# Edge columns of a convolution left out, input loads moved to another queue, statistics rows put in fewer DMAs, and second-phase expansions spread out, in a ConvNeXt-V2 block

## Chip, cores and metric

The kernel runs on one core of a Trainium2 chip. The metric is device time in microseconds (us), the median of several executions. No slow run occurred, and all kernels gave the reference's result. Ratios: the mean time of one kernel's runs over the mean of the other's of the same rounds, with a 95% interval; that is not quite the ratio of the medians that are quoted beside it.

The engines are called TensorE (PE in the profile, PEld its weight loads), VectorE (DVE), ScalarE (ACT), GpSimd (POOL) and SyncE (SP). SyncE does no arithmetic here: it only issues DMAs.

## The reference, cut to what matters

```python
# x: (1, 512, 512, 96) bf16; dw: (3, 3, 96); w1: (96, 384); w2: (384, 96)
xp = jnp.pad(x, ((0,0),(1,1),(1,1),(0,0)))
out = sum(xp[:, i:i+H, j:j+W, :] * dw[i, j] for i, j in 3x3)   # depthwise convolution
h = layernorm(out, axis=-1)
h = gelu_tanh(h @ w1)                                           # 384 channels
gx = sqrt((h * h).sum(axis=(1, 2)) + 1e-6)                      # over all pixels: GRN
nx = gx / (gx.mean(axis=-1) + 1e-6)
h = gamma * (h * nx) + beta + h
return x + h @ w2
```

The sum over all pixels splits the work in two. Phase 1 must see the whole picture before any output can be made; phase 2 multiplies by `w2`, whose rows by then carry the scale.

## The kernel before

The picture is cut into 128 blocks of 4 rows (2048 pixels). Phase 1 runs one *slot* for each block, software-pipelined: load x, transpose it, 3x3 convolution as 32x32 diagonal matmuls, statistics, normalization, a trip of the normalized block `yn` through DRAM to change its layout, expansion to 384 channels, gelu, sums of squares. For most blocks the gelu output is made again in phase 2 from `yn`; for the others it is stored (`g_dram`). The parts that the change and the argument touch:

```python
        def load_x(b):
            t = xinpool.tile([128, SL, C], bf16, name="xin")
            off = x.offset + b * GR * W * C
            if b in (0, NBLK - 1):
                pool.memset(t[:, 0:SL:SL - 1, :], 0.0)
        # ... (cut)
            else:
                act.dma_start(out=t[:].rearrange("p g c -> p (g c)"),
                              in_=bass.AP(x.tensor, off - C, [[PXP * C, 128], [1, SL * C]]))
            xins[b] = t

        def turn_x(b):
            xin = xins.pop(b)
            t = xt_ring[b % NXT]
            pairs = t[:, 0:2, :].rearrange("p i s -> p (i s)").bitcast(f32)
            dve.transpose(out=pairs.rearrange("p (g m) -> p g m", m=MB),
                          in_=xin[:, :, 0:64].bitcast(f32))
            dve.transpose(out=t[:, 2, :].rearrange("p (g m) -> p g m", m=MB), in_=xin[:, :, 64:96])
            flat = t[:].rearrange("p i s -> p (i s)")
            n = SL * MB
            for c0, c1 in ((0, 2), (2 * n - 2, 2 * n + 1), (3 * n - 1, 3 * n)):
                pool.memset(flat[:, c0:c1], 0.0)
        # ... (cut)

            def tap(n):
                k = sum(len(ms) for ms in mms[:n])
                mm = None
                for j, a, i, dx in mms[n]:
                    r = b * GR + j + a - 1
                    q = r % GR
                    c0 = MB * (1 + dx)
                    if mm is None and n in (3, 6):
                        pe.drain()
                    mm = pe.matmul(
                        Y[32 * j:32 * j + 32, i, :],
                        lhsT=Wd[32 * q:32 * q + 32, i, 3 * a + dx + 1, :],
                        rhs=x_row(r // GR, q, i, c0),
                        start=first[i, j] == k,
                        stop=last[i, j] == k,
                    )
                    k += 1
```

`load_x` issues its DMA from ScalarE. `turn_x` lets GpSimd zero the edge columns of the transposed block; the taps of the convolution (`tap`) read 512 columns from it.

Each batch of four blocks has its reciprocal standard deviations written to DRAM as rows (four DMAs) and read back as a broadcast, again four DMAs, one for each row of the blocks, 32 partitions each. `stage_write` stores `yn`, with the 4 rows as the slowest dimension of the DRAM side; `stage_read` brings it back with 96 channels on the partitions.

```python
        def stage_rows(k):
            b0, n = BATCHES[k]
            rt = rts.pop(k)
            N = n * GR * NG
            dst = r_dram[b0:b0 + n].rearrange("b r (g m) -> (b r g) m", g=NG)
            nq = min(32, N)
            with nc.allow_non_contiguous_dma("small rows of rstd"):
                for a in range(4):
                    sp.dma_start(
                        out=dst[:, 32 * a:32 * a + 32].rearrange("(t q) p -> q t p", q=nq),
                        in_=rt[32 * a:32 * a + nq, :(N + 31) // 32 * 32].rearrange("q (t p) -> q t p", p=32))

        def stage_bcast(k):
            b0, n = BATCHES[k]
            rbc = rbcpool.tile([128, BATCH, W], bf16, name="rbc")
            for j in range(GR):
                sp.dma_start(out=rbc[32 * j:32 * j + 32, :n, :],
                             in_=r_dram[b0:b0 + n, j, :].partition_broadcast(32))
            rbcs[k] = rbc
        # ... (cut)
        def stage_write(b):
            sp.dma_start(out=yn_dst(b), in_=yns.pop(b)[:])

        def stage_read(b):
            t = yn_ring[b % NYT]
            sp.dma_start(out=t[:C], in_=yn_src(b))
            ynts[b] = t
```

In the slot loop, all stores of a finished block (up to three of 512 KB) are issued together:

```python
        for s in range(last_slot + 1):
            get = lambda kind: at.get((s, kind), [])
            for b in get("write"):
                stage_write(b)
            for b in get("read"):
                stage_read(b)
            for k in get("bcast"):
                stage_bcast(k)
            if s + 3 < NBLK:
                load_x(s + 3)
            for f in stores:
                f()
            stores = []
        # ... (cut)
                b = mlp[0]
                expand, expand_px, squares, store = mlp_units(b)
                if pm_rows(b):
                    us = [lambda j=j: expand(j, 0) for j in range(NCH)] + [lambda n=n: expand_px(n) for n in range(3)]
                else:
                    us = [lambda j=j, i0=i0: expand(j, i0) for j in range(NCH) for i0 in (0, 2)]
                for f in bursts[0]:
                    f()
                us[0]()
                us[1]()
                squares(0)
                stores.append(lambda f=store: f(0))
                for f in bursts[1]:
                    f()
```

In phase 2 a recomputed block has its four expansions (three matmuls of 512 columns and one gelu each) made one block ahead, in the gaps of the block before; the loads are issued from GpSimd, SyncE and ScalarE.

```python
            g = gld.tile([128, NCH, GR * W], bf16, name="gl")
            ynt = None
            if not is_recomp(q):
                for j in range(NCH):
                    (nc.gpsimd, nc.sync, nc.scalar)[j].dma_start(out=g[:, j, :], in_=g_dram[q, j])
            else:
                ynt = ynld.tile([C, GR, W], bf16, name="ynl")
                nc.scalar.dma_start(out=ynt[:], in_=yn_src(q))
            xr = xrpool.tile([128, PXP, C], bf16, name="xr")
            nc.gpsimd.dma_start(out=xr[:], in_=x[0, r0:r0 + GR].rearrange("r w c -> (r w) c").rearrange(
                "(p g) c -> p g c", g=PXP))
            grp[q] = dict(g=g, ynt=ynt, xr=xr)
        # ... (cut)
        def stage_mm2(q, units):
            g, xb = grp[q]["g"], grp[q]["xb"]
            o_sb = opool.tile([128, PXP, C], bf16, name="o_sb")
            for sub in range(NSUB):
                O = psO.tile([128, GPS, C], f32, name="O")
                for gl_ in range(GPS):
                    gg = sub * GPS + gl_
                    for j in range(NCH):
                        nc.tensor.matmul(O[:, gl_, :], lhsT=g[:, j, gg * 128:(gg + 1) * 128], rhs=W2s[:, j, :],
                                         start=(j == 0), stop=(j == NCH - 1))
                nc.vector.tensor_tensor(out=o_sb[:, sub * GPS:(sub + 1) * GPS, :], in0=O[:],
                                        in1=xb[:, sub * GPS:(sub + 1) * GPS, :], op=ALU.add)
                if units:
                    units.pop(0)()
            grp.pop(q)
            return o_sb
        # ... (cut)
        PRE = 4
        nth = lambda n: ORDER[n] if n < NBLK else None
        for n in range(min(PRE, NBLK)):
            stage_load(ORDER[n])
        stage_xb(ORDER[0])
        for u in recompute_units(nth(0)):
            u()
        held = None
        for n, q in enumerate(ORDER):
            if n + PRE < NBLK:
                stage_load(ORDER[n + PRE])
            stage_xb(nth(n + 1))
            o_sb = stage_mm2(q, recompute_units(nth(n + 1)))
            if held:
                stage_out(*held)
            held = (q, o_sb)
        stage_out(*held)
```

## Time and profile before

| | before |
|---|---|
| median of 3 runs (lowest to highest) | 1909.8 us (1894.3 to 1910.1) |
| convolution stage of phase 1 (first to last evacuation of a convolution) | 25.7 to 1173.7 us, 9.04 us a slot |
| end of phase 1 ("drain": last blocks, final statistics) | 1173.7 to 1274.1 us, 100 us |
| phase 2 | 1274.1 to 1905.3 us, 631 us |

The first fence is from the page of the profiled run. Part 1 gives busy time, share of the span and number of instructions for each engine. Part 2 cuts the span into 40 slices: a digit is the busy share in tenths, PEclk the granted clock of TensorE in tenths of full speed, DMA the busy share of the 16 DMA engines, GB/s what they moved.

```profile
PE 1574.0 (83%) x28354; PEld 911.0 (48%) x28354; DVE 1152.7 (60%) x2022; ACT 1356.5 (71%) x1227; POOL 1381.3 (73%) x1355
...
PEclk9889989998999989999989999989999999999999
DMA  3346666665666666666566654569999999999995
GB/s 79 104 149 188 204 198 194 206 210 182 213 201 202 189 213 191 226 220 191 197 212 205 209 188 161 199 213 317 316 317 312 317 312 308 313 310 314 313 318 195
...
q10 hardware_dynamic: 34272, 111.16, 18.4%
```

About two thirds of the span (slices 1 to 26) move some 200 GB/s at a DMA share of 0.6; the rest moves 313 GB/s at 0.9 to 0.95. These are the two phases. q10 is ScalarE's queue; the others, not shown, are those of SyncE (q1) and GpSimd (q0).

The next fence is the table of stretches: the stretch, its length, busy us of each engine with the number of instructions, then granted clock, DMA share and GB/s. The first row is the whole convolution stage, the second 200 us of phase 2.

```profile
core 0: us, PE busy (x) PEld busy (x) DVE busy (x) ACT busy (x) POOL busy (x), PEclk, DMA share, GB/s
25.70:1173.70 1148.00, 965.91 (x20538) 512.90 (x20537) 784.15 (x1292) 796.77 (x793) 844.36 (x1020) 0.93 0.60 192
1400.00:1600.00 200.00, 170.63 (x2275) 113.31 (x2273) 85.61 (x162) 156.27 (x115) 155.55 (x95) 1.00 0.95 313
```

TensorE is busy 965.9 of 1148 us in the convolution stage, and idle 182 us. No other engine is fuller.

What the engines waited for between 200 and 1000 us (who waited, for whom, total us, times, longest us):

```profile
POOL yn L34 <- DMA rbc<-r_dram: 54.0, 11, 6.9
PE U L34 <- ACT gt L34: 53.6, 54, 3.5
ACT gt L34 <- DMA r_dram<-rt: 29.6, 11, 5.0
ACT gt L34 <- DMA yn_dram<-yn: 27.4, 4, 7.1
PE Y L34 <- POOL xT L34: 24.0, 16, 2.8
```

ScalarE's gelu (`ACT gt`) waits for two DMAs here that it has no data from (and for two more, 14.3 and 10.5 us, further down the list). They are waits of its own x loads, which stand ahead of the gelu in ScalarE's order: in the trace 111 of the 132 load instructions have waits for one or two of eight DMA semaphores before them, on which the `yn` stores, the rstd rows and other transfers land too. The timeline of ScalarE around one such stall (start, us, engine, operation; in brackets the idle time before it and what ended it):

```profile
612.92 1.96 ACT L34 ACTIVATE gm<-U 128x1024 bf16<-128x1024 f32 x2
621.52 0.36 ACTq L34 DMA_DIRECT2D xin<-in_x_dram  x1
621.98 1.94 ACT L34 ACTIVATE gt<-U 128x1024 bf16<-128x1024 f32 x2 [7.10 <-DMA yn_dram<-yn]
```

The x load could be issued only at 621.52, when a `yn` store had landed, and the gelu behind it started 7.10 us late.

### The profile page before, as it was taken

How to read it: one execution, taken by the hardware profiler on the slowest of the kernel's cores; microseconds unless marked ns; L12 is line 12 of the kernel's file. 1: busy time of each engine (PE TensorE's matmuls, PEld its weight loads, DVE VectorE, ACT ScalarE, POOL GpSimd, SP SyncE). 2: the span in 40 equal slices, each digit the busy share in tenths (PEclk: the TensorE clock that was granted, in tenths of full speed). 3: DMA queues.
4: the chain of work that ended last, by engine and by line, in shares of the span. 5: the costliest groups of instructions: out<-in, count | busy, mean ns of one | idle time of the engine just before them, and what ended most of it. 6: DMA issues, size and time to landing. Idle time of an engine off the chain costs nothing.

```text
span 1905.3 us, 64704 instructions
## 1 busy us (share of the span) xinstructions
PE 1574.0 (83%) x28354; PEld 911.0 (48%) x28354; DVE 1152.7 (60%) x2022; ACT 1356.5 (71%) x1227; POOL 1381.3 (73%) x1355
## 2 busy tenths in 40 slices
PE   5788888888898889888888878658888888888887
PEld 2334444444454445444444444335555555555555
DVE  5356766776677677767867767774444444444444
ACT  0165777776777778777767768857777877777776
POOL 4667777687777777867767876447777777777775
PEclk9889989998999989999989999989999999999999
DMA  3346666665666666666566654569999999999995
GB/s 79 104 149 188 204 198 194 206 210 182 213 201 202 189 213 191 226 220 191 197 212 205 209 188 161 199 213 317 316 317 312 317 312 308 313 310 314 313 318 195
DMA packets 188634, 433.75 MB, mean 228 GB/s; under 512 B 31712, under 2 KB 97344, under 8 KB 188352
## 3 DMA queue, kind: packets, MB, share of 16 engines
q1 hardware_dynamic: 138528, 248.98, 39.0%
q10 hardware_dynamic: 34272, 111.16, 18.4%
q0 software_dynamic: 15552, 69.48, 11.8%
q8 instruction: 222, 3.64, 0.8%
q14 instruction: 60, 0.49, 0.1%
HBM read 268.59 MB, written 160.96 MB: 225 GB/s over the span
## 4 chain that ended last, share of the span: by engine, by line
PE 27%; ACT 25%; DMA 20%; DVE 11%; POOL 7%; issue 5%; SPq 2%; ACTq 1%; POOLq 0%; DVEq 0%
ACT gl L696 12%; PE O L724 10%; DMA ynT<-yn_dram 8%; DVE bst L34 7%; ACT gl L703 6%; PE U L34 6%; ACT gt L34 5%; PE Y L34 5%; DMA yn_dram<-yn 5%; DMA rbc<-r_dram 4%; PE U L694 3%; PE SG L34 3%; POOL yn L34 2%; SPq L34 2%; DVE xT L34 2%
## 5 line engine op out<-in xcount | busy, mean ns | idle before, releaser
L34 DVE BATCH_NORM_STATS2 bst<-gt 128x6 f32<-128x512 bf16 x984 | 602.2, 674 | 296.3 <-ACT gt L34 295.9
L34 ACT ACTIVATE gt<-U 128x1024 bf16<-128x1024 f32 x492 | 478.3, 1028 | 269.2 <-PE U L34 113.9
L726 DVE TENSOR_TENSOR o_sb<-O,xb 128x384 bf16<-128x384 f32 x512 | 271.9, 555 | 355.7 <-PE O L724 355.5
L696 ACT ACTIVATE gl<-U 128x1536 bf16<-128x1536 f32 x264 | 374.9, 1455 | 152.7 <-PE U L694 152.7
L712 POOL TENSOR_TENSOR xb<-xr,B2bc_f 128x1536 f32<-128x1536 bf16 x126 | 393.0, 3119 | 100.6 <-DVE o_sb L726 99.4
L34 PE MATMUL Y<-xT,Wd 32*32 32x512 bf16 x13806 | 384.8, 408 | 92.7 <-POOL xT L34 35.2
L34 POOL TENSOR_TENSOR yn<-y_bf,rbc 128x1536 bf16<-128x1536 bf16 x128 | 396.6, 3100 | 87.9 <-DMA rbc<-r_dram 82.9
L34 PE MATMUL U<-ynT,w1p 128*128 128x512 bf16 x1008 | 294.6, 398 | 92.4 <-ACT gt L34 79.6
L34 POOL TENSOR_TENSOR ysq<-y_bf 128x1536 bf16<-128x1536 bf16 x128 | 351.9, 2750 | 16.2 <-ACT y_bf L34 16.2
L724 PEld LDWEIGHTS <-gl 128*128 128x128 bf16 x6048 | 285.6, 98 | 152.2 <-ACT gl L703 92.1
L724 PE MATMUL O<-W2s,gl 128*128 128x96 bf16 x6048 | 313.2, 206 | 49.4 <-ACT gl L703 48.8
L34 PEld LDWEIGHTS <-Wd 32*32 32x32 bf16 x13806 | 163.1, 90 | 284.7 <-issue 233.0
L34 ACT ACTIVATE gm<-U 128x1024 bf16<-128x1024 f32 x264 | 261.0, 1034 | 11.0 <-PE U L34 10.9
L694 PE MATMUL U<-ynl,w1p 96*128 96x512 bf16 x792 | 226.9, 379 | 42.3 <-ACT gl L696 40.2
L34 ACT ACTIVATE y_bf<-Y 128x1536 bf16<-128x1536 f32 x105 | 152.8, 1455 | 87.0 <-PE Y L34 70.1
L34 PEld LDWEIGHTS <-w1p 128*128 128x128 bf16 x1008 | 81.9, 99 | 252.7 <-issue 205.8
L34 DVE STREAM_TRANSPOSE xT<-xin 128x576 f32<-128x576 f32 (+1 forms) x256 | 181.3, 748 | 0.0
L34 PE MATMUL U<-w1p,ynT 128*128 128x384 bf16 (+2 forms) x1056 | 159.9, 287 | 20.1 <-ACT gt L34 12.4
L34 POOL MEMSET xT<- 128x2 bf16 (+2 forms) x384 | 26.5, 103 | 199.0 <-DVE xT L34 197.2
L34 PEld LDWEIGHTS <-ynT 128*128 128x128 bf16 x1056 | 90.7, 102 | 112.4 <-issue 83.2
L34 PE MATMUL SG<-gm 128*128 128x128 bf16 x2112 | 134.5, 221 | 0.8 <-issue 0.8
L703 ACT ACTIVATE gl<-U 128x1536 bf16<-128x1536 f32 x88 | 128.2, 1457 | 0.0
(83 smaller groups left out, 926.9 us busy)
## 6 DMA issues: line engine op xcount, KB each, us to landing
g_dram<-gt SPq DMA_DIRECT2D x114, 512.0 KB
xin<-in_x_dram ACTq DMA_DIRECT2D x126, 432.0 KB
yn_dram<-yn SPq DMA_DIRECT2D x128, 384.0 KB
ynT<-yn_dram SPq DMA_DIRECT2D x128, 384.0 KB
out_dram<-o_sb SPq DMA_DIRECT2D x128, 384.0 KB
xr<-in_x_dram POOLq DMA_DIRECT2D x126, 384.0 KB, 5.3
ynl<-yn_dram ACTq DMA_DIRECT2D x88, 384.0 KB
gl<-g_dram SPq DMA_DIRECT2D x38, 512.0 KB
```

The lines of the kernel that those rows point to most:

```text
L34: r = f(*a, **k)
L694: nc.tensor.matmul(U[:, i, :], lhsT=w1p[:C, j * 128:(j + 1) * 128], rhs=ynt[:, i, :], start=True, stop=True)
L696: nc.scalar.activation(out=perm_view(g[:, j, :], 0, 3), in_=perm_src(U[:]), func=ACTF.Gelu_apprx_tanh)
L703: nc.scalar.activation(out=g[:].rearrange("p j (g r m) -> p r j g m", g=PXP, r=GR, m=MB)[:, 3], in_=perm_src(U[:]), func=ACTF.Gelu_apprx_tanh)
L712: nc.gpsimd.tensor_tensor(out=xb[:], in0=grp[q]["xr"][:], in1=B2bc_f[:, None, :].to_broadcast([128, PXP, C]), op=ALU.add)
L724: nc.tensor.matmul(O[:, gl_, :], lhsT=g[:, j, gg * 128:(gg + 1) * 128], rhs=W2s[:, j, :], start=(j == 0), stop=(j == NCH - 1))
L726: nc.vector.tensor_tensor(out=o_sb[:, sub * GPS:(sub + 1) * GPS, :], in0=O[:], in1=xb[:, sub * GPS:(sub + 1) * GPS, :], op=ALU.add)
```

## The change

The change has six parts, in two phases.

1. Edge columns of the convolution are left out: taps at the left and right edge write 511 columns, so GpSimd's three memsets per block (384 in all) go away.
2. x loads move from ScalarE's queue to SyncE's.
3. The rstd rows of a batch go out in two DMAs for four, and come back in **one** broadcast DMA for four ("2+1").
4. Stores of gelu blocks are issued one a slot.
5. In phase 2 no load is issued from ScalarE.
6. In phase 2 the expansions are spread evenly over all blocks, a whole block (four units) ahead, with TensorE, VectorE and ScalarE held to program order. Blocks are loaded five ahead for four, into six buffers for five.

The diff also gives half-size gelu tiles of phase 1 a pool of their own (`gth` for `gt`), which is not shown here.

The diff, cut to its core:

```diff
-                act.dma_start(out=t[:].rearrange("p g c -> p (g c)"),
+                sp.dma_start(out=t[:].rearrange("p g c -> p (g c)"),
                               in_=bass.AP(x.tensor, off - C, [[PXP * C, 128], [1, SL * C]]))
... (cut)
-            flat = t[:].rearrange("p i s -> p (i s)")
-            n = SL * MB
-            for c0, c1 in ((0, 2), (2 * n - 2, 2 * n + 1), (3 * n - 1, 3 * n)):
-                pool.memset(flat[:, c0:c1], 0.0)
... (cut)
+                    o0, o1 = max(0, -dx), W - max(0, dx)
+                    c0 = MB * (1 + dx) + o0
                     if mm is None and n in (3, 6):
                         pe.drain()
                     mm = pe.matmul(
-                        Y[32 * j:32 * j + 32, i, :],
+                        Y[32 * j:32 * j + 32, i, o0:o1],
                         lhsT=Wd[32 * q:32 * q + 32, i, 3 * a + dx + 1, :],
-                        rhs=x_row(r // GR, q, i, c0),
+                        rhs=x_row(r // GR, q, i, c0, o1 - o0),
                         start=first[i, j] == k,
                         stop=last[i, j] == k,
... (cut)
-            dst = r_dram[b0:b0 + n].rearrange("b r (g m) -> (b r g) m", g=NG)
-            nq = min(32, N)
+            nq, nt = min(32, N), (N + 31) // 32
             with nc.allow_non_contiguous_dma("small rows of rstd"):
-                for a in range(4):
-                    sp.dma_start(
-                        out=dst[:, 32 * a:32 * a + 32].rearrange("(t q) p -> q t p", q=nq),
-                        in_=rt[32 * a:32 * a + nq, :(N + 31) // 32 * 32].rearrange("q (t p) -> q t p", p=32))
+                if nq == 32:
+                    for t in range(nt):
+                        sp.dma_start(
+                            out=r_dram[b0:b0 + n].rearrange("b r w -> (b r w)").rearrange(
+                                "(t q a p) -> t a q p", q=32, a=4, p=32)[t],
+                            in_=rt[:, 32 * t:32 * t + 32])
... (cut)
-            for j in range(GR):
-                sp.dma_start(out=rbc[32 * j:32 * j + 32, :n, :],
-                             in_=r_dram[b0:b0 + n, j, :].partition_broadcast(32))
+            sp.dma_start(out=rbc[:, :n, :].rearrange("p n w -> p (n w)"),
+                         in_=bass.AP(r_dram[b0].tensor, r_dram[b0].offset, [[n * W, GR], [0, 32], [1, n * W]]))
... (cut)
-            for f in stores:
-                f()
-            stores = []
+            if stores:
+                stores.pop(0)()
... (cut)
             else:
                 ynt = ynld.tile([C, GR, W], bf16, name="ynl")
-                nc.scalar.dma_start(out=ynt[:], in_=yn_src(q))
+                nc.sync.dma_start(out=ynt[:], in_=yn_src(q))
             xr = xrpool.tile([128, PXP, C], bf16, name="xr")
... (cut)
-                if units:
-                    units.pop(0)()
+                        pe2.matmul(O[:, gl_, :], lhsT=g[:, j, gg * 128:(gg + 1) * 128], rhs=W2s[:, j, :],
+                                   start=(j == 0), stop=(j == NCH - 1))
+                dve2.tensor_tensor(out=o_sb[:, sub * GPS:(sub + 1) * GPS, :], in0=O[:],
+                                   in1=xb[:, sub * GPS:(sub + 1) * GPS, :], op=ALU.add)
+                pace(n, sub)
... (cut)
-        PRE = 4
+        PRE = 5
+        UPB = NCH + 1
+        LEAD = UPB
+        todo = [n for n, q in enumerate(ORDER) if is_recomp(q) for _ in range(UPB)]
+        total = len(todo)
+        made = [0]
+        waiting = []
+
+        def advance(target, upto):
+            while made[0] < total and made[0] < target and todo[made[0]] < upto:
+                n = todo[made[0]]
+                if not waiting:
+                    waiting.extend(recompute_units(ORDER[n]))
+                waiting.pop(0)()
+                made[0] += 1
+
+        def pace(n, sub):
+            due = sum(1 for v in todo if v <= n + 1) if sub == NSUB - 1 else 0
+            even = LEAD + (n * NSUB + sub + 1) * total / (NSUB * NBLK)
+            advance(max(due, even), n + PRE)
+
... (cut)
-        for u in recompute_units(nth(0)):
-            u()
+        advance(LEAD, PRE)
```

## The prediction

> **What bounds it now.** Two phases. Phase 1 (conv, norm, expansion, statistics; 0 to 1260 us) runs slots of about 9.1 us (66 squares on GpSimd in 600 us, the table of stretches). TensorE is busy 85% there at a granted clock of 0.94, ScalarE 75%, VectorE 72%, GpSimd 74%. Phase 2 (1290 to 1905 us) has TensorE 85%, ScalarE 78%, the DMA engines 95% at 313 GB/s.
>
> In phase 1 the DMA share is only 0.64, but the packet records show a lopsided load: three or more packets are in flight 96% of the time, with peaks at 4 to 5 and at 16. The yn store (4x96x512 against 128 partitions) moves its 1 KB packets with about a quarter of the engines busy. [...] So four "hot" engines carry every yn store. By the median packet times (1 KB 46 ns, 3456 B 135 ns, 4 KB 159 ns), their work per slot, an estimate: yn store 96x46 = 4.4 us, xin 1.1, ynT 0.95, g 1.1, rstd broadcast 0.4: 8.0 us of 9.1, or about 95% with the slow packets in the mean. Long landings (yn store up to 13 us) stall ScalarE through its own DMA issues (list of waits: gelu behind r_dram, ynT, yn_dram, rbc: about 125 us), and TensorE waits 92 us for gelu.
>
> **What the change does.**
> - Edge memsets: 384 x 103 ns leave GpSimd, with its 197 us of waiting for the transposes, and TensorE's 35 us wait for them. Conv columns 511 for 512: nothing.
> - ScalarE loses its DMA stalls (up to 125 us, of which TensorE saw perhaps 60).
> - g stores are spread: fewer 1.5 MB bursts.
> - The rstd broadcast becomes one DMA whose source has slowest dimension 4[...]. Per batch of 4 slots: 32 packets of 4 KB x 159 ns = 5.1 us for 32 x 46 ns = 1.5 us before; rows add 0.4. So the hot engines get about 1.0 us more per slot: 9.0 us at median packet times (estimate), nearer 9.7 with slow packets. This is a floor: what ScalarE and GpSimd gain cannot be collected, and phase 1 becomes bound by four DMA engines: +65 us.
> - Startup: xin is issued after 19 SyncE loads (10 us of issues): included, about +7 us.
> - Phase 2: expansions a block ahead take away TensorE's waits for gelu (49 + 40 us). But the DMA engines are at 95%; 5% of 600 us is all there is: -25 us.
>
> Sum: 1909.8 + 65 - 25 = 1950 us; 80% range 1875 to 2030. Faster by over 2%: 0.17; within 2%: 0.33; slower: 0.50.
>
> **What would show it.** Right: slot 9.4 to 9.9 us; the broadcast's packets 4 KB with a quarter of the engines; concurrency 4 to 5 more often; ScalarE's waits for DMA gone, but VectorE's transposes or TensorE's expansions waiting for xin or ynT; SyncE lagging. Phase 2 about 590 us with DMA 97% or more and the waits for gelu small. Wrong: broadcast on 16 engines, slot below 8.8 us, granted clock nearer 1.
>
> **What would make it wrong.** If slow packets come from two queues interleaving, one queue may be quicker and phase 1 stays at 9.1 us or falls; if the broadcast spreads over 16 engines, phase 1 gains 60 us or more; if phase 2's DMA can go above 330 GB/s, it gains up to 50 us; if one in-order queue delays xin behind waiting issues, it is slower still.

The sum came to 1909.8 + 65 - 25 = 1950 us. Two things in it were the author's estimate: that the merged broadcast would move on a quarter of the engines, and that this would be the same quarter that carries the `yn` stores (its "hot engines"). The 1.0 us more a slot, and with it the +65, rest on both. For the `yn` store the trace of before shows the quarter: from 667.75 to 668.75 us, with mostly 4 of its 1 KB packets in flight and hardly anything else, the DMA share is 0.27. For the broadcast the trace of after shows it, below. No trace numbers the engines.

## The result

| | before | after |
|---|---|---|
| median us (lowest to highest, 4 runs each) | 1909.95 (1894.3 to 1910.9) | 1833.71 (1818.95 to 1840.3) |
| convolution stage | 1148.0 us, 9.04 a slot | 1107.6 us, 8.72 a slot |
| drain | 100.4 us | 122.6 us |
| phase 2 | 631.2 us | 573.5 us |
| mean granted clock over the span | 0.955 | 0.949 |

The ratio is 0.961 (0.953 to 0.969): faster by about 4%, 75 us of span. The predicted 1950 us was on the wrong side; the range began at 1875. About 18 us came from phase 1 and 58 us from phase 2. About 6 us of the longer drain lie in the new program order: expansions stand ahead of the first output matmul on TensorE, which starts at 1256.4 though the scale was summed at 1248.5 (7.9 us later; before, 1.6 us).

The same parts of the page after:

```profile
PE 1536.7 (84%) x28172; PEld 922.8 (50%) x28354; DVE 1163.8 (64%) x2022; ACT 1366.3 (75%) x1227; POOL 1358.4 (74%) x971
...
PEclk9899999999999989999999999897999999999998
DMA  3355666666666666665666665558999999999983
GB/s 82 99 153 190 206 214 193 207 219 217 201 210 203 205 199 209 206 210 196 214 216 202 208 205 178 169 200 255 359 379 369 351 343 337 360 375 365 356 290 133
```

ScalarE's queue q10, 18.4% of the engines' span before, is gone from the page. Most slices of phase 2 now show 337 to 379 GB/s, where before they stood at 308 to 318.

The table of stretches after (same columns; the trace lacks some 170 matmul records of the convolution stage, about 8 us of busy time at 46 ns each):

```profile
core 0: us, PE busy (x) PEld busy (x) DVE busy (x) ACT busy (x) POOL busy (x), PEclk, DMA share, GB/s
26.20:1133.80 1107.60, 941.93 (x20366) 507.18 (x20538) 783.97 (x1289) 798.27 (x793) 820.08 (x644) 0.95 0.60 196
1400.00:1600.00 200.00, 181.78 (x2563) 132.51 (x2561) 98.90 (x183) 174.19 (x126) 175.71 (x105) 0.97 1.00 350
```

The waits after, 200 to 1000 us:

```profile
POOL yn L34 <- DMA rbc<-r_dram: 183.4, 22, 9.9
...
DVE xT L34 <- DMA xin<-in_x_dram: 80.7, 30, 5.6
...
PE Y L34 <- DVE xT L34: 49.0, 24, 4.9
```

TensorE's 53.6 us of waiting for gelu have become 1.6 (further down this list), and its 24 us for the edge memsets are gone. In their place VectorE's transposes wait 80.7 us for x itself, TensorE 49.0 us for the transposes, and the normalization on GpSimd 183.4 us for the rstd broadcast (54.0 before). So the old stalls were removed and a new one was made: data now comes late on SyncE's queue. Two stretches of 2 us show the new broadcast in flight:

```profile
720.00:722.00 2.00, 1.79 (x43) 0.84 (x42) 0.66 (x2) 1.97 (x3) 0.00 (x0) 1.00 0.26 107
722.00:724.00 2.00, 2.00 (x45) 1.78 (x44) 0.00 (x0) 2.00 (x3) 0.00 (x0) 1.00 0.28 112
```

The DMA share (second number from the right) is 0.26 to 0.28 while the broadcast moves: a quarter of the engines carry it, and the packet records show 4 KB packets there. That is the quarter that the prediction had counted on. Which engines they are, the trace doesn't show. But from 722.25 to 724 us packets of an x load (3456 B) are in flight beside those of the broadcast, and even so only 4 or 5 of SyncE's queue are in flight together.

### The profile page after: what moved, and what is told of

It reads as the page before. It is cut to its first block, busy times and chain, and to the rows that moved or that the text cites. A ratio compares the mean times of both kernels' runs of the same rounds, so it can differ in the third digit from the quotient of the medians.

```text
span 1829.9 us, 63713 instructions
## 1 busy us (share of the span) xinstructions
PE 1536.7 (84%) x28172; PEld 922.8 (50%) x28354; DVE 1163.8 (64%) x2022; ACT 1366.3 (75%) x1227; POOL 1358.4 (74%) x971
## 4 chain that ended last, share of the span: by engine, by line
POOL 40%; issue 20%; PE 17%; DMA 13%; ACT 5%; DVE 3%; SPq 1%; another core or an unknown queue 0%; ACTq 0%; DVEq 0%; POOLq 0%
POOL yn L34 17%; POOL ysq L34 17%; PE O L34 9%; PE U L34 8%; DMA out_dram<-o_sb 6%; ACT gl L34 4%; DMA gl<-g_dram 4%; POOL nt L34 3%; POOL var L34 2%; DVE bst L34 2%; DMA rbc<-r_dram 1%; DMA yn_dram<-yn 1%; PE Y L34 1%; DVE o_sb L34 1%; POOL rn L34 1%
## 5 line engine op out<-in xcount | busy, mean ns | idle before, releaser
L34 ACT ACTIVATE gl<-U 128x1536 bf16<-128x1536 f32 x352 | 489.9, 1450 | 94.5 <-PE U L34 89.0
L34 ACT ACTIVATE gth<-U 128x1024 bf16<-128x1024 f32 x264 | 261.0, 1025 | 200.2 <-issue 154.3
L34 PEld LDWEIGHTS <-gl 128*128 128x128 bf16 x6048 | 301.6, 99 | 148.4 <-ACT gl L34 41.1
L34 PE MATMUL O<-W2s,gl 128*128 128x96 bf16 x6048 | 324.8, 209 | 55.7 <-ACT gl L34 30.2
L34 DVE BATCH_NORM_STATS2 bst<-gth 128x6 f32<-128x512 bf16 x528 | 326.0, 671 | 50.9 <-ACT gth L34 50.8
L34 PE MATMUL U<-ynT,w1p 128*128 128x512 bf16 x851 | 285.2, 406 | 49.8 <-DMA ynT<-yn_dram 14.5
L34 DVE BATCH_NORM_STATS2 bst<-gt 128x6 f32<-128x512 bf16 x456 | 276.2, 676 | 78.5 <-ACT gt L34 78.4
L34 PE MATMUL U<-ynl,w1p 96*128 96x512 bf16 x1056 | 293.6, 387 | 3.1 <-DMA ynl<-yn_dram 1.6
L34 PEld LDWEIGHTS <-w1p 96*128 96x128 bf16 (+1 forms) x2064 | 165.6, 100 | 255.2 <-issue 154.4
L34 ACT ACTIVATE gt<-U 128x1024 bf16<-128x1024 f32 x228 | 220.8, 1031 | 61.6 <-remote 45.1
```

The lines of the kernel that those rows point to most:

```text
L34: r = f(*a, **k)
```

## Experiments

Fifteen runs followed, of thirteen new kernels (the changed kernel itself, and it with the memsets back, each ran twice). All outputs are right. Gains given in us are the ratio's distance from 1 times about 1905 us, or differences of such. The question after the result was: phase 1 did not become slower, so was the floor of four engines wrong, and what did each part of the change bring? The theory of the prediction was that four DMA engines bound phase 1 already before, so that no stall taken away could be collected. The rival was that before was bound by stalls of ScalarE and GpSimd as TensorE saw them, and that the merged broadcast was a new cost added to real gains. In the quoted texts the letters of theories are those of each text; what follows from each run is told in words. Where the texts of rbc16, xin_edge, yn16_rbc16 and yn_rows said on how many engines a DMA of 32 or 128 partitions runs, that is cut: no record of this study counts the engines of such a DMA.

A table of the convolution stage, from the table of stretches of each kernel, serves all of them. Every kernel executes the same some 20,540 matmuls there, and their busy time goes up with the time at half clock (932.0 us with 58 in rbc16, 983.3 with 188 in rows_only). The last column is the time in which the clock record of the trace stands at half speed.

| kernel | stage, us | TensorE busy | TensorE idle | at half clock |
|---|---|---|---|---|
| before | 1148.0 | 965.9 | 182.1 | 150 |
| rows_only | 1179.4 | 983.3 | 196.1 | 188 |
| xin_sp | 1077.8 | 946.5 | 131.3 | 79 |
| xin_edge | 1042.9 | 935.1 | 107.8 | 68 |
| after (some records missing) | 1107.6 | 941.9 | 165.7 | 113 |
| rbc16 | 1038.9 | 932.0 | 106.9 | 58 |
| yn16_rbc16 | 1076.4 | 949.0 | 127.5 | 99 |
| yn_rows | 1059.7 | 943.3 | 116.4 | 68 |

### Phase 1 alone, phase 2 alone

p1_only has the new phase 1 with the old phase 2, p2_only the reverse; the diff is the change cut at this line:

```diff
     with ExitStack() as p2:     # above: phase 1 of one kernel; below: phase 2 of the other
```

> The change's phase 1 with the phase 2 of before. Theory A (the gain is mostly phase 2, and phase 1 only breaks even because the four engines that carry the yn store and the broadcast are full): 20 to 30 us faster than before (ratio about 0.985), with the end of phase 1 at about 1235 us as in the change. Rival B (the two phases help each other, for instance through one queue for everything): under 5 us or over 45 us.

Measured: 1876.2 us, ratio 0.985 (0.982 to 0.989), about 28 us faster. The number is that of theory A, but it was set after the result was known, and A's reason (phase 1 "only breaks even" because four engines are full) is not tested by it.

> Phase 1 of before with the change's phase 2. Theory A: 50 to 60 us faster than before (ratio about 0.97), phase 2 taking about 573 us for 631 us, DMA above 340 GB/s, together with p1_only making up the whole 76 us. Rival B: the sum of the two parts misses the whole by more than 15 us.

Measured: 1848.2 us, ratio 0.970 (0.967 to 0.974), about 57 us faster. The two gains add up to 85 us; the whole change measured 75 to 76. So phase 1 gained where a loss of 65 had been predicted, and phase 2 gained more than twice the predicted 25.

### The broadcast split into four again

rbc16 is the changed kernel with the one broadcast DMA split again into four of 32 partitions:

```diff
-            sp.dma_start(out=rbc[:, :n, :].rearrange("p n w -> p (n w)"),
-                         in_=bass.AP(r_dram[b0].tensor, r_dram[b0].offset, [[n * W, GR], [0, 32], [1, n * W]]))
+            for j in range(GR):
+                sp.dma_start(out=rbc[32 * j:32 * j + 32, :n, :].rearrange("p n w -> p (n w)"),
+                             in_=bass.AP(r_dram[b0].tensor, r_dram[b0].offset + j * n * W, [[0, 32], [1, n * W]]))
```

> The changed kernel, but the rstd broadcast again as four DMAs, each with a slowest dimension of 32 [...]. Theory A (phase 1 of the changed kernel is bound by four full DMA engines): their work falls from 9.0 to about 8.0 us per slot, phase 1 shortens by 40 to 90 us against the changed kernel, packets in flight 3 or more less than 99% of the time, ratio to before 0.92 to 0.94. Rival C (phase 1 is bound by TensorE and ScalarE taking turns, the DMA load is only a bystander): within 10 us of the changed kernel, ratio about 0.96.

Measured: 1744.4 us, ratio 0.916 (0.913 to 0.919). This is about 89 us less than the changed kernel (from the medians; 86 to 88 from the ratios; they ran on different chips, and each beside the kernel before), from one DMA. The pieces are 4 KB in both, so it is not the size of the packets that cost. It is the best version and beats both kernels. Its convolution stage in the table of stretches (columns as before):

```profile
26.00:1064.90 1038.90, 931.99 (x20539) 505.36 (x20538) 783.45 (x1293) 796.81 (x793) 826.26 (x646) 0.97 0.65 210
```

TensorE is idle 107 us, where the changed kernel had 166. In its list of waits (200 to 1000 us) the transposes' wait for x is gone, and TensorE's wait for them fell from 49.0 to 4.0 us. The normalization on GpSimd still waits 127 us for the broadcast, and little of that is seen at TensorE: GpSimd is busy 826 of 1039 us there. The expectation's theory A had 0.92 to 0.94, so the gain was a little larger than that.

### The merged rows and broadcast alone

rows_only is the kernel before with part 3 of the change only (the hunk of `stage_rows` and `stage_bcast` above, and the column order of the statistics that it needs).

> The kernel before with only the rstd rows and broadcast in 2+1 DMAs. Theory A (the merged broadcast loads the four engines that the yn store already fills, a cost hidden inside the change): 20 to 90 us slower than before, packets in flight 3 or more above 98% of the time. Rival D (fewer DMAs help by themselves, and the cost seen in rbc16 comes only together with one queue): within 15 us of before, or faster.

Measured: 1949.6 us against 1903.4, ratio 1.024 (1.023 to 1.026): 46 us slower. Taken alone this part is a clear loss. Its waits, 200 to 1000 us:

```profile
ACT gt L34 <- PE U L34: 192.4, 86, 9.0
POOL yn L34 <- DMA rbc<-r_dram: 162.8, 22, 12.2
PE Y L34 <- POOL xT L34: 74.2, 27, 6.9
```

TensorE's wait for the edge memsets rose from 24.0 to 74.2 us. The memsets stand in GpSimd's order with the normalization, which now waits 162.8 us for the broadcast (54.0 before), so a late broadcast makes the memsets late as well; that chain is read from the two lines, not tested by itself. ScalarE's waiting for TensorE is what follows.

### x loads off ScalarE's queue, alone

```diff
-                act.dma_start(out=t[:].rearrange("p g c -> p (g c)"),
+                sp.dma_start(out=t[:].rearrange("p g c -> p (g c)"),
                               in_=bass.AP(x.tensor, off - C, [[PXP * C, 128], [1, SL * C]]))
```

> The kernel before with only the x loads of phase 1 moved from ScalarE's to SyncE's queue. Theory E (ScalarE's gelus stand behind x loads that wait for other DMAs' semaphores, and this is most of phase 1's loss): 30 to 70 us faster than before, ScalarE's waits for DMAs gone, granted clock in phase 1 above 0.95. Rival: under 15 us, because the g stores in bursts of three now delay x in the same queue, or because the memsets hold the convolution.

Measured: 1837.8 us, ratio 0.965 (0.963 to 0.967): 66 us faster from the queue of one load.

Its convolution stage in the table of stretches, and the line of its waits (200 to 1000 us) that had been 53.6 us:

```profile
26.00:1103.80 1077.80, 946.46 (x20537) 503.40 (x20537) 784.58 (x1293) 797.27 (x794) 847.08 (x1021) 0.96 0.62 203
```

```profile
PE U L34 <- ACT gt L34: 2.3, 3, 1.7
```

TensorE waits for gelu 2.3 us. This run refutes the floor as it was predicted for the kernel before. The `yn` stores and the broadcast go as before, and the packet records show the same cover (three or more packets in flight 96% of the time between 400 and 1000 us, in both), yet a slot takes 8.49 us instead of 9.04. So 96% cover was not a limit. The 1 KB packets averaged 55 ns before and 52 ns here, with a median of 46: their slow tail was not a fixed price either.

The table above shows something more. Of the 70 us that the stage lost, 51 are idle time of TensorE and 19 are busy time: its instructions ran faster, with 79 us at half clock for 150. The section after the experiments comes back to this.

### Memsets and edge columns

Four runs put a price on part 1. Three are the changed kernel, or rbc16, with the memsets and the 512 columns back:

```diff
+            for c0, c1 in ((0, 2), (2 * n - 2, 2 * n + 1), (3 * n - 1, 3 * n)):
+                pool.memset(flat[:, c0:c1], 0.0)
...
-                    o0, o1 = max(0, -dx), W - max(0, dx)
+                    o0, o1 = 0, W
```

> rbc16 with the edge memsets and full 512 columns of before. Theory H (before's 35 us wait of TensorE for the memsets was on the critical path, since GpSimd does them between 3 us operations): 15 to 35 us slower than rbc16's 0.916, so a ratio to before of 0.924 to 0.934, TensorE waiting 25 us or more for GpSimd's xT. Rival: under 8 us, the waits move to the transposes.

Measured (rbc16 with the memsets): 1773.0 us, ratio 0.931 (0.926 to 0.936), against 0.916 for rbc16: about 29 us, compared over two chips by way of the kernel before.

> The changed kernel with the edge memsets and full columns of before; in rbc16 the same edit cost about 0.015 of the time before. Theory M (with the merged broadcast the four DMA engines are the floor, so what GpSimd saves can't be collected): under 10 us slower than the changed kernel, a ratio to before of 0.959 to 0.966. Rival N (the memsets cost what they cost, whatever the DMA engines do): 20 to 35 us slower, 0.972 to 0.98.

Measured (after with the memsets, 5 rounds): 1845.0 us, ratio 0.970 (0.968 to 0.972). It fell between the two expectations and was inconclusive alone, because after itself had not run on that chip. So both ran again on one chip, in the same rounds:

> The changed kernel once more, only to have its ratio on the same chip as the next two: 0.955 to 0.966.

> after_memset once more beside the changed kernel. Theory M (the four engines swallow what the memsets cost): within 8 us of after_again. Rival N: 20 us or more slower. Between: the floor is soft and swallows a part.

Measured: after 1830.7 us, ratio 0.962 (0.959 to 0.966); with memsets 1847.7 us, 0.971 (0.968 to 0.974). The memsets cost about 16 us (by the two intervals, give or take 9) while the broadcast is one DMA, which moved at a DMA share of 0.26 to 0.28 in after.

xin_edge goes the other way: xin_sp with part 1 added, broadcast still as before, in four DMAs. In the trace of before these were not held to a quarter: between 400 and 1000 us, within 6 us of each of their 68 issues, 15 to 21 packets of 1 KB are in flight at the peak (those of a `yn` store among them; in after, where `yn` stores alone have that size, 3 to 7 is the peak after their issues). From 663.25 to 665.50 us, while a broadcast moves, the DMA share is 0.72.

> Before with the x loads on SyncE's queue and the edge columns left out, broadcast and stores as before. Theory M: the memsets' cost is collected here[...]: 20 to 35 us faster than xin_sp's 0.965, so 0.945 to 0.955. Rival: within 8 us of xin_sp, so the memsets cost only where the g stores and rows are changed too.

Measured: 1802.3 us, ratio 0.946 (0.944 to 0.949), against 0.965 for xin_sp: about 35 us (give or take 7). So part 1 brings some 29 to 35 us where the broadcast goes in four DMAs, and 16 us where it goes in one. The 16 and the 35 differ by more than the noise; the 16 and the 29 (give or take 11) do not. This is what is left of the floor that the prediction spoke of: after the change, roughly half of this gain is swallowed, not all of it. That the load of the quarter of the engines swallows it is argued; the broadcast also comes later there, and x loads stand behind it in SyncE's order, and no run tells these apart.

### Stores in bursts

rbc16_burst is rbc16 with all stores of a block issued in one slot again:

```diff
-            if stores:
-                stores.pop(0)()
+            for f in stores:
+                f()
+            stores = []
```

> rbc16 with a block's three g stores issued together at the next slot, as before. Theory (with one queue in order, a burst of 1.5 MB stands before xin and the yn store): 10 to 30 us slower than rbc16, ratio 0.921 to 0.932, and waits for xin come back. Rival: within 6 us of rbc16, since the bytes are the same.

Measured: 1748.2 us, ratio 0.918 (0.915 to 0.922), within the intervals the same as rbc16's 0.916. Spreading the stores brought nothing that can be seen; my expectation of a gain missed.

### Phase 2: queues or order

q2_only is before with part 5 alone; spread_act is the kernel before with part 6 and the deeper buffers, but the loads still on ScalarE:

```diff
-                    (nc.gpsimd, nc.sync, nc.scalar)[j].dma_start(out=g[:, j, :], in_=g_dram[q, j])
+                    (nc.gpsimd, nc.sync, nc.sync)[j].dma_start(out=g[:, j, :], in_=g_dram[q, j])
...
-                nc.scalar.dma_start(out=ynt[:], in_=yn_src(q))
+                nc.sync.dma_start(out=ynt[:], in_=yn_src(q))
```

> The kernel before with only phase 2's loads moved from ScalarE's to SyncE's queue. Theory F (phase 2 gains by the expansions' order, and the DMA share of 95% was no ceiling): within 15 us of before, DMA still about 315 GB/s. Rival G (one hardware queue less is what lets the DMA engines go faster): 25 us or more faster.

Measured: 1902.5 us, ratio 0.999 (0.997 to 1.001): nothing.

> Phase 1 of before, the change's phase 2 but its loads still on ScalarE's queue. Theory F: 30 to 60 us faster than before, DMA above 335 GB/s with three queues, the waits of TensorE for the fourth gelu mostly gone. Rival G: under 20 us faster, DMA stays below 325 GB/s.

Measured: 1848.9 us, ratio 0.971 (0.969 to 0.974), the same as p2_only's 0.970 and so the whole gain of phase 2. TensorE's waits for the gelus of the expansions, 1350 to 1750 us, before and then in spread_act:

```profile
PE O L724 <- ACT gl L703: 30.8, 57, 0.5
PE U L694 <- ACT gl L696: 26.0, 53, 0.5
```

```profile
PE O L34 <- ACT gl L34: 12.4, 10, 1.9
...
PE U L34 <- ACT gl L34: 0.4, 1, 0.4
```

They fell from 56.8 to 12.8 us. The stretch that stood at 313 GB/s, and then the whole of phase 2, before and in spread_act:

```profile
1400.00:1600.00 200.00, 192.83 (x2789) 141.48 (x2787) 106.99 (x199) 189.45 (x137) 184.87 (x112) 1.00 1.02 377
```

```profile
1274.10:1905.30 631.20, 535.55 (x7199) 359.08 (x7199) 272.13 (x514) 482.09 (x352) 477.04 (x283) 1.00 0.92 305
1276.50:1849.70 573.20, 516.15 (x7189) 375.66 (x7187) 277.63 (x512) 485.67 (x350) 477.12 (x282) 0.97 0.93 332
```

In that stretch the loads and stores now run at 377 GB/s at a DMA share of 1.02, with TensorE busy 192.8 of 200 us. A DMA share of 0.95 before was not a ceiling. The 377 and the changed kernel's 350 are not to be compared with each other, since the same 200 us lie on different parts of phase 2: over the whole phase both kernels take 573 us at 332 GB/s. A share above 1 also says that packets overlap: in spread_act, for 29% of these 200 us, more than 16 packets other than instruction packets were in flight on the 16 engines, so a packet's time is not time that an engine gives to it alone. How little the busy share says here is shown by the two kernels: over the whole of phase 2, at shares of 0.92 and 0.93, they moved 305 and 332 GB/s. The order and the lead of the expansions is what made the difference; which of the two (or the forced program order, or the deeper buffers), no run tells apart.

### The yn store in other forms

If the four engines still bind phase 1 in rbc16, the `yn` store, their largest load (4.4 of 8.0 us in the prediction's estimate), should go next. yn16_rbc16 splits it into four DMAs of 32 partitions:

```diff
-            sp.dma_start(out=yn_dst(b), in_=yns.pop(b)[:])
+            yn = yns.pop(b)
+            for r in range(GR):
+                sp.dma_start(out=yn_dst(b)[r], in_=yn[32 * r:32 * r + 32])
```

> rbc16, and the yn store also as four DMAs of 32 partitions [...]. Theory A: the work of the fullest DMA engine falls to about 4.7 us per slot, so phase 1 ends where the next limit lies (TensorE, 85% busy now): slots of 7.6 to 8.3 us, 70 to 140 us less than the changed kernel, ratio to before 0.89 to 0.93. Rival C: within 10 us of the changed kernel.

Measured: 1782.3 us, ratio 0.935 (0.932 to 0.938), 38 us **slower** than rbc16. The cover by three or more packets (400 to 1000 us) fell from 99% to 79%, and the time went up. (The 4.7 us of the expectation is an estimate that takes the store to be spread over all 16 engines; that it is was not shown.) A second way keeps one DMA of 128 partitions, with `yn` stored row by row in DRAM (reads then in pieces of 1 KB):

```diff
-    yn_dram = dram.tile([NBLK, C, GR * W], bf16, name="yn_dram")
+    yn_dram = dram.tile([NBLK, GR, C, W], bf16, name="yn_dram")
...
-            sp.dma_start(out=yn_dst(b), in_=yns.pop(b)[:])
+            sp.dma_start(out=yn_dst(b), in_=yns.pop(b)[:].rearrange("p i w -> p (i w)"))
```

> rbc16 with yn kept row by row in DRAM, so that its store is one DMA of 128 partitions with 3072 bytes each [...] and its loads take 1 KB pieces. Theory K (yn16_rbc16 lost 38 us to rbc16 because it issued four DMAs a slot where one had been): the fullest engine is relieved without more DMAs, phase 1 is 15 to 50 us shorter than rbc16's 1169 us, phase 2 up to 10 us longer, ratio 0.89 to 0.915. Rival L (relieving the four engines brings nothing more once the broadcast has left them; the next limit is TensorE's own rhythm): phase 1 within 10 us of rbc16's, or longer.

Measured: 1766.1 us, ratio 0.927 (0.924 to 0.930), 22 us slower than rbc16, with a cover of 74%. So lowering the cover further brought no gain over rbc16. Where the time went can be read from the list of TensorE's waits between 26 and 1060 us, here of rbc16 and then of yn16_rbc16 ("issue" is idle time with no wait that the profile shows):

```profile
PE Y L34 <- DVE y_bf L34: 20.1, 11, 2.8
PE Y L34 <- issue: 15.6, 15, 2.8
PE SG L34 <- issue: 11.9, 10, 2.4
```

```profile
PE Y L34 <- issue: 36.5, 25, 4.0
PE Y L34 <- DVE y_bf L34: 17.3, 10, 2.8
PE SG L34 <- issue: 9.9, 8, 3.5
```

The two "issue" lines grew from 27.5 to 46.4 us (49.3 over the whole stage of yn16_rbc16), about as much as the 21 us that TensorE's idle time grew by. The other 17 us of the longer stage are busy time, with 99 us at half clock instead of 58. What the "issue" gaps are can only be guessed from the packet records: between 200 and 1000 us, all 27 of them over 0.3 us in yn16_rbc16 (37.4 us), all 32 in yn_rows and all 18 in rbc16 (21.9 us) end 2.1 to 3.0 us after the start of a 16 KB packet of the queue marked "instruction" (as do 4 of 4 before, 8 of 9 in xin_sp and 14 of 15 after). By chance it would be about one in seven: 124 such packets started in these 800 us of rbc16, and most of them were followed by no such gap. That TensorE waits for such a packet in these gaps is a guess from this timing alone; nothing was run to test it, and why the gaps grow with the `yn` store in the other forms stays open.

## A stall is paid twice

The prediction counted each stall once. The clock record says that this is too little. These are six neighbouring stretches of the kernel before, 3.41 us each, laid on the edges at which the clock changes (columns as before; the clock is the third number from the right):

```profile
611.05:614.47 3.42, 2.59 (x79) 1.66 (x56) 3.42 (x7) 3.42 (x4) 2.86 (x8) 1.00 0.67 260
614.47:617.88 3.41, 1.44 (x17) 0.44 (x16) 1.42 (x3) 0.41 (x1) 3.06 (x9) 1.00 0.54 176
617.88:621.29 3.41, 1.61 (x37) 0.57 (x37) 0.00 (x0) 0.00 (x0) 3.41 (x2) 0.50 0.34 112
621.29:624.71 3.42, 1.65 (x6) 0.61 (x5) 1.67 (x3) 2.50 (x3) 0.88 (x1) 0.50 0.71 177
624.71:628.12 3.41, 3.30 (x46) 1.53 (x45) 3.30 (x6) 2.75 (x4) 2.50 (x4) 0.50 1.08 257
628.12:631.53 3.41, 3.41 (x88) 2.60 (x87) 0.00 (x0) 1.92 (x3) 3.41 (x2) 1.00 0.37 98
```

Two gaps of TensorE lie here: 2.66 us until 616.44, waiting for the edge memsets, and 3.46 us until 623.06, waiting for the gelu behind the ScalarE stall shown above. In the stretch at 614.47 TensorE is busy 1.44 of 3.41 us, at 617.88 and 621.29 1.61 and 1.65 us; the clock is 0.50 in each stretch *after* one of these, the last time at 624.71, when TensorE is full again. At 628.12 it is back. The timeline shows the price on the same work, 36 convolution matmuls:

```profile
610.50 0.91 PE L34 MATMUL Y<-xT,Wd 32*32 32x512 bf16 x36
...
618.10 1.50 PE L34 MATMUL Y<-xT,Wd 32*32 32x512 bf16 x36
...
625.09 1.50 PE L34 MATMUL Y<-xT,Wd 32*32 32x512 bf16 x36
```

They take 0.91 us at full clock and 1.50 at half clock. The lengths in the clock record are regular: every stretch of it but the last is a multiple of 3.41 us, at 1.0 or 0.5. In six kernels (before, after, rbc16, yn16_rbc16, rows_only, xin_sp), between 200 and 1000 us, the clock fell 95 times; in 91 of them TensorE had been busy at most 57% of the 3.41 us before, and no such 3.41 us with less than 46% passed without a fall. A short gap was enough: of the first one above, 2.0 us lay in the stretch at 614.47, and the next stretch stands at half clock.

This is why the two columns of the table move together. From before to xin_sp, idle time fell by 51 us and busy time by 19, with 71 us less at half clock; from before to rows_only, both rose.

## Why the prediction was wrong

**The step that failed** is this one: "This is a floor: what ScalarE and GpSimd gain cannot be collected, and phase 1 becomes bound by four DMA engines: +65 us", with its basis "nearer 9.7 with slow packets".

- *Before was not at a floor.* The prediction took 96% cover by three or more packets, and a sum of "about 95% with the slow packets in the mean", as proof that the four engines were full. xin_sp has the same cover and the same stores and gains 66 us. Cover says that something is always under way there, not that it could not go faster.
- *The size of the floor after the change.* At median packet times the prediction had 9.0 us a slot; the changed kernel runs 8.72 us, with three or more packets in flight 99.9% of the time (rbc16 has 99% at 8.18 us). The step up to 9.7, for slow packets, was the mis-sized term. In the changed kernel the 1 KB packets average 48 ns, near the median of 46; x's packets average 195 for a median of 135, and those of 4 KB 184 for 159. An estimate by the prediction's own count, with these mean times, gives about 10 us of work in a slot of 8.72, and for rbc16 about 9.0 in 8.18. So times of packets that are in flight together can't be added up as if an engine served one after another, and their sum is no floor.
- *The gains could be collected.* The raw gains were well sized: "perhaps 60" of ScalarE's stalls measured 66 us (70 in the stage: 51 of idle time and 19 of clock), and 35 us for the memsets measured 29 to 35. The account of phase 1, from ratios times about 1905 us: x loads -67, edge columns -35, together -102, against a measured -28. The difference, +74, is what is left for the merged rows and broadcast; it lies between the 46 us measured alone and the 89 us where everything else is quick. The merged broadcast was a loss, as predicted; but it was a loss *set against* gains, not a floor that cancels them. Taking xin_edge's gain (0.054) and that of phase 2 alone (0.030) together gives 0.916, which is rbc16's ratio: the merged rows, the spread stores and the new tile pool show nothing of their own.
- *Phase 2.* "But the DMA engines are at 95%; 5% of 600 us is all there is" failed by the same confusion of busy with full. Over the whole phase the rate rose from 305 to 332 GB/s, in the changed kernel and in spread_act alike, and 25 us became 57. The prediction had named this itself among what would make it wrong: "if phase 2's DMA can go above 330 GB/s, it gains up to 50 us".

What was right: the broadcast on a quarter of the engines (a DMA share of 0.26 to 0.28) in 4 KB packets; ScalarE's waits for DMAs gone; VectorE's transposes and then TensorE waiting for x instead; the cost of the broadcast as a thing to fear. A slot of 9.4 to 9.9 us was wrong, and the listed counter-sign, "slot below 8.8 us", is what came.

What stays open: why the two kernels with other forms of the `yn` store are slower. The accounts close (idle time without a visible wait, plus half clock), but the cause of the gaps is argued from timing alone. It is also not shown how much of the phase 2 gain is order and how much is lead.

## What to carry to other kernels

Before you merge small DMAs, look at how many engines the merged one moves on: here the broadcast as one DMA with a slowest dimension of 4 moved at a DMA share of 0.26 to 0.28, a quarter of the engines, and four DMAs of 32 partitions were 89 us faster. Don't let an engine that computes issue a load that may have to wait: here a gelu behind an x load on ScalarE started 7.10 us late, and moving these loads was worth 66 us. A stall can cost twice: after TensorE's gap of 2.66 us, the work of 0.91 us took 1.50 at half clock. And before you call a resource a floor, take away a stall that has nothing to do with it and see whether the time moves: a DMA busy share of 95% in one phase and a cover of 96% in the other were both no ceiling here.
